# Weights of experts 1 and 2 as casting loads on GpSimd's DMA queue, in place of fp32 staging and GpSimd copies; x group loads issued two units sooner

## The chip, the cores and the metric

The kernel runs on one core of one Trainium2 chip. The metric is device time in microseconds (us); lower is better.

Engine names in the profile: PE is TensorE (matmul), PEld its weight load, DVE is VectorE, ACT is ScalarE, POOL is GpSimd, SP is SyncE, which here does nothing but issue DMAs; "SPq" is the issuing of DMAs on it. "L464" is line 464 of that kernel. From the point where the change deletes or adds lines on, the numbers of the two kernels differ by one or more.

## The reference, cut to what matters

```python
# attention with 8 batches, 8 heads, 512 local + 32 global tokens, head size 64
x = attention output, reshaped to [4352 tokens, 512]   (8 x 544)

logits = x @ w_gate                        # 8 experts
P = np.exp(logits - logits.max())
for _ in range(8):                         # Sinkhorn: needs the logits of ALL tokens
    P /= P.sum(1, keepdims=True) + 1e-09
    P /= P.sum(0, keepdims=True) + 1e-09
    P *= N / E
out = 0
for e in range(8):
    h = np.maximum(x @ w1[e], 0.0)         # w1[e]: 512 x 1024, fp32
    out += P[:, e:e+1] * (h @ w2[e])       # w2[e]: 1024 x 512, fp32
```

The routing `P` mixes all tokens, so nothing that uses it can start before the gate logits of the last token are there.

## The kernel before: the parts that matter

The kernel has four stages. Attention takes roughly the first 185 us. Routing (eight short iterations on VectorE, with one tiny matmul each) follows. Expert 0 is computed without scaling by `P`, so its matmuls need no routing: PE uses them as filling work inside attention and under the routing. After that come two passes over experts 1 to 3 and 4 to 7, in 119 units of 6.2 us by the kernel's own plan.

The attention output goes through DRAM. GpSimd's queue stores it, SP's queue reads it back transposed.

The weights of experts 1 and 2 are loaded under the second half of attention, as fp32 into a staging tile, and GpSimd copies them to fp16. The weights of expert 3 already come by a DMA that casts on the way; in this kernel all such DMAs are issued by GpSimd.

```python
def fetch(e, i, pool):            # 512 KB of fp32 on SP's queue; 3 staging buffers during attention, 2 later
    t = stg[e, i] = pool.tile([P, F], FP32, tag="w0s" if pool is ld else "s", bufs=3 if pool is ld else 2, ...)
    nc.sync.dma_start(out=t, in_=moe_w1[e, P * i : P * (i + 1)])          # or two blocks of w2
def settle(e, i, pool):           # the cast, on GpSimd
    nc.gpsimd.tensor_copy(out=ws[e][0][...], in_=t...)                    # i < 4; two copies for w2

def fetch_cast(e, i, pool):       # expert 3: fp32 in DRAM to fp16 in SBUF in one DMA
    nc.gpsimd.dma_start(out=ws[e][0][...], in_=moe_w1[e, ...])            # i < 4; two such for w2
```

The order of instructions on every engine is decided when the kernel is built, by a small scheduling model in it. The dependency called "seen" (the last load of v has been issued) is only used by that model. It orders the emission and puts no wait into the program.

The softmax here doesn't subtract the row's maximum and nothing guards it: scores larger than these inputs give would overflow.

Of the kernel before, what the change touches and what calls it, by code (L numbers as in the profile page):

```python
# [10 lines left out]
FP32 = mybir.dt.float32  # L11
# [6 lines left out]
def kernel(  # L18
# [13 lines left out]
    nc = tc.nc  # L32
# [4 lines left out]
    F = moe_w1.shape[2]  # L37
    S = Sg + Sl
    NTOK = B * S
    P = 128  # L40
# [33 lines left out]
    Dhalf, FK, DK = D // 2, FT // 2, DP // 2  # L74
# [4 lines left out]
    ws = {}  # L79
# [6 lines left out]
    def new_w(e, i, pool, tag=""):  # L86
        if i == 0:
            ws[e] = [pool.tile([P, 4, DK, F // 2], FP16, tag="w1r" + tag, bufs=1, name="w1r"), None, None]
        elif i == 8:
            ws[e][1] = pool.tile([P, 7, FK, Dhalf], FP16, tag="wb" + tag, bufs=1, name="wb")  # L90
# [61 lines left out]
    def op(eng, us, fn, key, deps=(), alloc=None, uses=(), lat=0.15):  # L152
        o = Op()
        o.eng = eng if isinstance(eng, dict) else {eng: us}
        o.pe = eng == "PE"
        o.fn, o.key, o.deps, o.alloc, o.lat, o.end = fn, key, [x for x in deps if x is not None], alloc, lat, None
        users[o] = [o]
        o.held, o.bw, o.nd = [o], 0.0, 1
        o.act, o.fill, o.after = 0, False, []
        for u in uses:  # L160
            if u is not None:
                users[u].append(o)
                o.deps.append(u)
        pending.append(o)
        return o
# [83 lines left out]
    PEL, DMAL = 0.28, 2.2  # L249
# [3 lines left out]
    ld = tc.alloc_tile_pool(name="ld", bufs=1)  # L253
# [14 lines left out]
    stage, nat, gst, late = {}, {}, {}, {}  # L268
# [288 lines left out]
    for m in range(NM):  # L557
        c = lo[m] - (P * m - WIN)
# [22 lines left out]
    def add_load(b, nm, n, of, key):  # L581
        h0, h1 = H * n // of, H * (n + 1) // of
        prev = b - 2 if b == 2 else b - 1
        deps = [] if b < 2 else [ops_cast[prev, nm, i] for i in range(parts_of(nm))]
        ops_load[b, nm, n] = dma(dma_us[nm] / of, lambda: load(b, nm, h0, h1), key, deps)
# [108 lines left out]
    for nm_ in ("q", "k"):  # L694
        add_load(1, nm_, 0, 1, 3.5)

    w0s = {}

    def load_w0(i):
# [21 lines left out]
    for b in range(B):  # L721
# [23 lines left out]
        for g, (t0, n) in enumerate(groups):  # L745
            if S_tok * b < P * (t0 + n) <= S_tok * (b + 1):
                k = HP * (b + 1) + 0.5
                if g >= GPE:
                    TG[g] = dma(2.0, lambda g=g: turn_group(g), k, [x for x in stored[b] + (stored[b - 1] if b else [])],
                                alloc=("xT", 4), lat=5.0, issue=1.4)  # L750
# [17 lines left out]
    for n, (kind, g, i) in enumerate(seq):  # L768
        key = 1000.0 + n
        if kind == "h":  # L770
            us = 0.435
            if i == 0:
                htag = op("NONE", 0.0, lambda: None, -5, w0[:4], alloc=("hT", 2))
            u0 = op("PE", us, lambda g=g, i=i: h_unit(g, i, 0), key, [*w0[:4], before, *BK[g]],
                    alloc=("mm", 2), uses=[TG[g]])
# [6 lines left out]
        else:  # L782
            prev = None
            for q in range(4):
                prev = op("PE", 0.435, lambda g=g, i=i, q=q: y_unit(g, i, q), key,
                          [before, *w0[4:], *([hops[g, f][1] for f in range(FT * groups[g][1] // GT)] if q == 0 else [prev])],
                          alloc=("mm", 2) if q == 0 else None, uses=[hops[g, 0][2]], lat=PEL if q == 3 else 0.0)
# [23 lines left out]
    opened = op("NONE", 0.0, open_late, -5, [psum])  # L811
# [44 lines left out]
    def load_group(n, g):  # L856
        x = xgs[n, g] = late["cp"].tile([P, 2, D], FP16, tag="xg", bufs=3, name="xg")
        nc.sync.dma_start(out=x, in_=xd[256 * g : 256 * (g + 1)].rearrange("(a p) d -> p a d", p=P))
# [24 lines left out]
    def take_x(eng, k):  # L883
        xps[k] = late["cp"].tile([P, DP, 256], FP16, tag="xp", bufs=5, name="xp")
        copy_on(eng, xps[k], xts[k])
# [82 lines left out]
    TU, SEMA = 6.2, 0.12  # L968
    OP = {("open", 0): opened, ("psum", 0): psum, ("routed", 0): chain[-1], **{("y", i): yops[0, i] for i in (0, 1)}}

    def mk(name, u, eng, us, fn, at, deps=(), uses=(), alloc=None, lat=None, bw=0.0):
        if lat is None:
            lat = {"PE": PEL, "NONE": 0.0}.get(eng, SEMA) if isinstance(eng, str) else SEMA
        OP[name, u] = op(eng, us, fn, at, [OP[d] for d in deps if d in OP], alloc, [OP[d] for d in uses if d in OP], lat)
        OP[name, u].bw = bw
# [30 lines left out]
    def add_prep(k):  # L1006
        n, g, e = work[k]
        at = TU * (k - 4.5)
        if e == PASSES[n][0] and ("LG", k) not in OP:
            mk("LG", k, "DMA", 0.45, lambda: load_group(n, g), at - 4 * TU, [("open", 0)], alloc=("xg", 3), lat=4.0, bw=0.8)  # L1010
        for a in (0, 1):
            mk(("SC", a), k, {"ACT": 0.58, "DVE": 0.26}, 0, lambda eng, a=a: scale_x(eng, k, a), at, [("routed", 0)],
               [("LG", k - PASSES[n].index(e))] + [(("SC", 0), k)] * a, alloc=("xs", 2) if a == 0 else None)
        if k < 2:
            mk("PT", k, "PE", 0.45, lambda: flip_x(k), at, [(("SC", 1), k)], [(("SC", 0), k)], ("xt", 1))
            OP["PT", k].act = 0
            mk("TX", k, {"ACT": 0.93, "DVE": 0.61}, 0, lambda eng: take_x(eng, k), at, [], [("PT", k)], ("xp", 5))
        else:
            mk("PX", k, "DMA", 0.45, lambda: put_x(k), at + 1.0, [(("SC", 1), k)], [(("SC", 0), k)], ("xsd", NX), lat=3.0, bw=0.8)
            mk("TX", k, "DMA", 1.25, lambda: turn_x(k), at + TU, [], [("PX", k)], ("xp", 5), lat=3.5, bw=1.2)  # L1020
        for n_ in (2, 3, 4):
            mk(("V", n_), k, "DVE", (0.335, 0.2, 0.2)[n_ - 2], lambda n_=n_: prep(k, n_), TU * (k - 1.5) + 0.01 * n_,
               [(("V", n_ - 1), k)], [("TX", k)], ("tt", 3) if n_ == 2 else None)
# [105 lines left out]
    def store_o(c, a):  # L1129
        nc.gpsimd.dma_start(out=(ya, outr)[c[0]][2 * c[1] + a], in_=obs[c][:, a, :])  # L1130

    stg = {}

    def fetch(e, i, pool):
        t = stg[e, i] = pool.tile([P, F], FP32, tag="w0s" if pool is ld else "s", bufs=3 if pool is ld else 2, name="stg")
        if i < 4:
            nc.sync.dma_start(out=t, in_=moe_w1[e, P * i : P * (i + 1)])
        else:
            nc.sync.dma_start(out=t.rearrange("p (k d) -> p k d", k=2),
                              in_=moe_w2[e, 2 * P * (i - 4) : 2 * P * (i - 3)].rearrange("(k p) d -> p k d", p=P))  # L1140

    def settle(e, i, pool):

        k, t = i % 4, stg[e, i]
        if i < 4:
            new_w(e, i, pool)
            nc.gpsimd.tensor_copy(out=ws[e][0][:, k // DK :: 2, k % DK, :], in_=t.rearrange("p (f x) -> p f x", f=2))
        else:
            if i == 4:
                new_w(e, 8, pool)  # L1150
            for c in (0, 1):
                nc.gpsimd.tensor_copy(out=ws[e][1][:, 2 * c + k // 2, 2 * (k % 2) : 2 * (k % 2) + 2, :],
                                      in_=t.rearrange("p (k c d) -> p c k d", k=2, c=2)[:, c])

    EARLY = 12

    def fetch_cast(e, i, pool):
        k = i % 4
        if i < 4:
            new_w(e, i, pool)  # L1160
            nc.gpsimd.dma_start(out=ws[e][0][:, k // DK :: 2, k % DK, :], in_=moe_w1[e, P * k : P * (k + 1)].rearrange("p (f x) -> p f x", f=2))
        else:
            if i == 4:
                new_w(e, 8, pool)
            for c in (0, 1):
                nc.gpsimd.dma_start(out=ws[e][1][:, 2 * c + k // 2, 2 * (k % 2) : 2 * (k % 2) + 2, :],
                                    in_=moe_w2[e, 2 * P * k : 2 * P * (k + 1), Dhalf * c : Dhalf * (c + 1)].rearrange("(k p) d -> p k d", p=P))

    def load_w_cast(e, pool):
        for i in range(8):  # L1170
            mk(("W", i), e, "POOL", 0.75 if i < 4 else 1.5, lambda i=i: fetch_cast(e, i, pool()), 900.0 + 0.01 * i,
               [("open", 0), (("W", i - 1), e)] + [(("W", i - 3), e)] * (i > 2), lat=3.5)
            if i:
                OP[("W", i), e].deps.remove(OP[("W", i - 1), e])
                OP[("W", i), e].after.append(OP[("W", i - 1), e])
        OP[("WL", 0), e], OP[("WL", 1), e] = OP[("W", 3), e], OP[("W", 7), e]

    def load_w(e, pool):
        for i in range(8):
            early = 8 * (e - 1) + i < EARLY  # L1180
            mk(("W", i), e, "DMA", 0.45, lambda i=i, early=early: fetch(e, i, ld if early else late["ec"]), 900.0 + e + 0.01 * i,
               [("seen", 0) if early else ("open", 0), (("W", i - 1), e) if i else (("W", 7), e - 1)], alloc=("w0s", 3) if early else ("stg", 2), lat=DMAL, bw=1.6)
            mk(("WC", i), e, "POOL", 0.95 if i < 4 else 1.1, lambda i=i: settle(e, i, pool()), 900.0 + e + 0.01 * i, [(("WC", i - 1), e)], [(("W", i), e)])
            if early:
                opened.deps.append(OP[("WC", i), e])
        OP[("WL", 0), e], OP[("WL", 1), e] = OP[("WC", 3), e], OP[("WC", 7), e]

    OP["seen", 0] = ops_load[B - 1, "v", 0]
    c0 = (0, 0)
    for e, pool in ((1, lambda: wA), (2, lambda: late["wD"]), (3, lambda: late["wB"])):  # L1190
        (load_w if e < 3 else load_w_cast)(e, pool)
    for e in (1, 2, 3):
        for n in range(4):
            mk(("C1", n), e, "DVE", 0.605, lambda e=e, n=n: combine_w1(e, n, late["cp" if e < 3 else "wB"], str(e) if e < 3 else ""),
# [4 lines left out]
    for k in range(5):  # L1199
        add_prep(k)  # L1200
# [61 lines left out]
```

## Time and profile before

| | before |
|---|---|
| median of 3 runs | 990.07 us (987.4 to 991.75) |
| profiled span | 986.6 us |
| PE busy | 960.9 us, 97% of the span |
| PE idle, 130 to 265 us (windows) | 135.00 - 130.91 = 4.1 us |
| transposed loads of xG (gate) and xT (expert 0) to landing, medians | 4.6 and 5.0 us |
| last step of the routing, start | 219.0 us |

First the page's line of PE in the kernel before: busy microseconds, share of the span, number of instructions.

```profile
PE 960.9 (97%) x12918; PEld 824.3 (84%) x12918; DVE 819.7 (83%) x2047; ACT 718.4 (73%) x1379; POOL 209.7 (21%) x406
```

Then its windows: bounds, length, busy time and instructions of each engine, granted TensorE clock (1.00 is full), mean DMA share (the time of packets of all queues over 16 engines' time, so it can pass 1), and GB/s.

```profile
130.00:265.00 135.00, 130.91 (x1456) 81.35 (x1452) 101.74 (x248) 84.19 (x167) 44.08 (x62) 1.00 0.87 225
265.00:375.00 110.00, 110.00 (x1496) 104.23 (x1494) 100.74 (x253) 86.85 (x163) 47.02 (x111) 1.00 0.97 194
375.00:600.00 225.00, 222.74 (x2998) 209.23 (x2996) 198.58 (x498) 179.31 (x336) 51.69 (x115) 1.00 0.86 191
...
150.00:175.00 25.00, 24.41 (x354) 13.87 (x351) 14.94 (x42) 17.54 (x38) 9.20 (x13) 1.00 0.78 203
175.00:200.00 25.00, 24.29 (x233) 12.65 (x234) 17.34 (x44) 13.24 (x29) 8.61 (x12) 1.00 0.85 231
200.00:232.00 32.00, 29.93 (x206) 16.97 (x205) 28.18 (x58) 16.86 (x29) 19.14 (x26) 1.00 1.05 269
```

PE is the bottleneck in every stretch shown, and full between 265 and 375 us.

The last piece is VectorE's timeline while GpSimd casts: two subtractions of the same shape (expert weights are combined once on arrival). GpSimd casts from 220.84 to 223.61 us, so the first stands beside casts for most of its length and the second beside none.

```profile
222.06 2.10 DVE L126 TENSOR_TENSOR w1r<-w1r 128x1024 f16<-128x1024 f16 x1
...
224.34 0.68 DVE L126 TENSOR_TENSOR w1x<-w1x,w1r 128x1024 f16<-128x1024 f16 x1
```

### The profile page before, as it was taken

To read this page: it belongs to the slowest core of one execution; us is meant where nothing else is said; L and a number is where in the kernel's file an instruction comes from. 1 tells how busy PE (TensorE), PEld (TensorE's weight loads), DVE (VectorE), ACT (ScalarE), POOL (GpSimd) and SP (SyncE) were. 2 spreads that over 40 slices of the span, in tenths; PEclk is the share of its full clock that TensorE was granted. 3 is DMA by queue.
4 is the path that set the end of the run, shared out by engine and by line. 5 is a ranking of instruction groups with operands and counts; after the bars stand their busy time and mean duration, and the time that the engine had idled before them with its cause. 6 is when DMAs were issued, how large, how long until landed. Compare 5 with 4: busy or idle time off the path is not lost.

```text
span 986.6 us, 31631 instructions
## 1 busy us (share of the span) xinstructions
PE 960.9 (97%) x12918; PEld 824.3 (84%) x12918; DVE 819.7 (83%) x2047; ACT 718.4 (73%) x1379; POOL 209.7 (21%) x406
## 2 busy tenths in 40 slices
PE   6899999998999999999999999999999999999998
PEld 3555655446999999999999989999999999999997
DVE  6888886689689989878888998888888888888876
ACT  5668676556777877877887787777777777777764
POOL 3411124352144443332320000000000000000000
PEclk9999999999999999999999999999999999999999
DMA  9999696898799998799886985555665555556621
GB/s 288 306 254 286 190 282 195 225 277 213 156 233 181 192 202 182 178 195 182 185 178 167 251 201 138 141 139 141 136 141 140 140 140 142 139 140 141 140 73 44
DMA packets 256098, 179.29 MB, mean 182 GB/s; under 512 B 158288, under 2 KB 236880, under 8 KB 255440
## 3 DMA queue, kind: packets, MB, share of 16 engines
q1 hardware_dynamic: 229872, 126.78, 54.1%
q0 software_dynamic: 24496, 50.09, 20.4%
q8 instruction: 101, 1.65, 0.7%
q10 hardware_dynamic: 1584, 0.39, 0.2%
q14 instruction: 45, 0.37, 0.1%
HBM read 91.24 MB, written 66.06 MB: 159 GB/s over the span
## 4 chain that ended last, share of the span: by engine, by line
PE 81%; DVE 8%; DMA 5%; ACT 3%; issue 3%; POOL 1%; SPq 0%; ACTq 0%; DVEq 0%; POOLq 0%
PE X L908 19%; PE Y L908 9%; PE acc_5045 L946 9%; PE acc_5046 L946 9%; PE acc_5043 L946 9%; PE Z L908 5%; PE py L534 5%; PE ph L518 5%; PE acc_5044 L946 4%; PE pt L302 1%; PE sc L328 1%; DVE h L129 1%; DMA w1r<-wd_7_87 1%; DVE o L129 1%; DMA xp<-xsd_83 1%
## 5 line engine op out<-in xcount | busy, mean ns | idle before, releaser
L922 ACT ACTIVATE h<-h 128x512 f16<-128x512 f16 x357 | 225.3, 631 | 109.9 <-DVE h L129 108.3
L908 PEld LDWEIGHTS <-w1r 128*128 128x128 f16 x3808 | 251.0, 98 | 14.9 <-issue 2.2
L908 PEld LDWEIGHTS <-w1x 128*128 128x128 f16 x2856 | 186.3, 98 | 8.7 <-issue 2.3
L946 PEld LDWEIGHTS <-s 128*128 128x128 f16 x1904 | 168.6, 98 | 12.9 <-issue 0.3
L908 PE MATMUL X<-tt,w1r 128*128 128x128 f16 x1904 | 145.1, 219 | 1.0 <-ACT u2s L919 0.9
L946 PE MATMUL acc_5046<-wb,s 128*128 128x256 f16 x952 | 142.3, 273 | 0.1
L946 PEld LDWEIGHTS <-h 128*128 128x128 f16 x1428 | 127.1, 98 | 9.9 <-issue 0.6
L129 DVE TENSOR_TENSOR h<-u2s,Y 128x512 f16<-128x512 f32 x119 | 81.5, 684 | 51.1 <-PE Y L908 51.1
L129 DVE TENSOR_TENSOR h<-u3s,Y 128x512 f16<-128x512 f32 x119 | 81.1, 682 | 9.4 <-PE Y L908 5.3
L129 DVE TENSOR_TENSOR h<-p1s,Z 128x512 f16<-128x512 f32 x119 | 81.4, 684 | 7.8 <-ACT p1s L919 2.2
L919 ACT COPY p1s<-X 128x512 f32<-128x512 f32 x119 | 69.5, 584 | 25.2 <-PE X L908 22.3
L1130 POOL DMA_DIRECT2D out_dram<-o x32 | 17.5, 547 | 307.0 <-DVE o L129 307.0
L919 ACT COPY u2s<-X 128x512 f32<-128x512 f32 x119 | 68.4, 574 | 16.6 <-PE X L908 16.4
L908 PE MATMUL Y<-tt,w1x 128*128 128x128 f16 x952 | 72.6, 219 | 1.6 <-DVE tt L126 1.0
L908 PE MATMUL Z<-xp,w1r 128*128 128x128 f16 x952 | 72.6, 219 | 1.3 <-DVE h L129 1.2
L866 ACT ACTIVATE xs<-xg,P_nat 128x512 f16<-128x512 f16 x100 | 71.8, 723 | 1.6 <-DMA xsd_81<-xs 1.6
L129 DVE TENSOR_TENSOR s<-h 128x512 f16<-128x512 f16 x119 | 50.1, 421 | 27.1 <-ACT h L922 27.0
L908 PE MATMUL X<-tt,w1x 128*128 128x128 f16 x952 | 72.6, 219 | 0.0
L908 PE MATMUL X<-xp,w1r 128*128 128x128 f16 x952 | 72.6, 219 | 0.0
L908 PE MATMUL Y<-xp,w1x 128*128 128x128 f16 x952 | 72.6, 219 | 0.0
L919 ACT COPY u3s<-X 128x512 f32<-128x512 f32 x119 | 68.7, 577 | 4.4 <-PE X L908 3.3
L946 PE MATMUL acc_5045<-wb,h 128*128 128x256 f16 x476 | 71.4, 273 | 0.4 <-DVE o L129 0.4
(725 smaller groups left out, 1902.7 us busy)
## 6 DMA issues: line engine op xcount, KB each, us to landing
y0d<-ys SPq DMA_DIRECT2D x34, 256.0 KB, 5.6
xg<-xd SPq DMA_DIRECT2D x34, 256.0 KB, 3.9
o<-y0d POOLq DMA_DIRECT2D x34, 256.0 KB, 4.5
ya<-o POOLq DMA_DIRECT2D x34, 256.0 KB, 3.2
o<-ya POOLq DMA_DIRECT2D x34, 256.0 KB, 4.0
stg<-in_moe_w_dram SPq DMA_DIRECT2D x16, 512.0 KB, 5.5
out_dram<-o POOLq DMA_DIRECT2D x32, 256.0 KB, 2.7
qs<-in_q_l_dram SPq DMA_DIRECT2D x7, 1024.0 KB, 7.9
```

The source lines that it names most:

```text
L129: nc.vector.tensor_tensor(out=o, in0=a, in1=b_, op=ALU.add)
L302: nc.tensor.transpose(pt[:, j, P * so : P * (so + 1)], nat[b, nm][:, so, 2 * hp : 2 * hp + 2, :], identity)
L328: nc.tensor.matmul(pss[p, m // 2, i][:, off[m] : off[m] + wid[m]], qkT[p][rr, 1, P * m : P * (m + 1)], qkT[p][rr, 0, lo[m] : hi[m]], start ...
L518: nc.tensor.matmul(phs[g, n][:, j], w1_0[:, dk, P * (w * n + j) : P * (w * n + j + 1)], xTs[g][:, dk, 0:TG], start=(dk == 0), stop=(dk == ...
L534: nc.tensor.matmul(pys[g, c], hTs[g][:, fk, P * c : P * (c + 1)], w2_0[:, fk, :], start=(fk == 0), stop=(fk == FT - 1))
L866: nc.scalar.activation(out=o, in_=i, func=AF.Copy, scale=w)
L908: nc.tensor.matmul(dst[:, j, :], l[:, d, P * j : P * (j + 1)], r[:, d, :], start=(first and j == 0 and d == 0), stop=(j == FK - 1 and d == ...
L919: nc.scalar.copy(out=d[k], in_=X[k])
L922: nc.scalar.activation(out=hq(k, f, t), in_=hq(k, f, t) if src is None else src, func=AF.Relu)
L946: nc.tensor.matmul(acc(i), l[:, j, :], wb[:, r, j, :], start=(e == es[0] and j == 0 and i in (1, 5)), stop=(e == es[-1] and j == FK - 1), ...
L1130: nc.gpsimd.dma_start(out=(ya, outr)[c[0]][2 * c[1] + a], in_=obs[c][:, a, :])
```

## The change

The intent: the casts are done by the DMA in flight, as for expert 3. The fp32 staging and 24 GpSimd copies go away, VectorE is no longer disturbed by them, and SP has 16 fewer loads to issue. Separately, the x group loads of the expert passes get an earlier key (the number by which the scheduling model orders the instructions).

```diff
-    def fetch(e, i, pool):      ... nc.sync.dma_start(out=t, in_=moe_w1[e, ...])        # fp32, staged
-    def settle(e, i, pool):     ... nc.gpsimd.tensor_copy(out=ws[e][0][...], in_=t...)
-    EARLY = 12
     ...
-    def load_w_cast(e, pool):
+    def load_w(e, pool):
         for i in range(8):
-            mk(("W", i), e, "POOL", 0.75 if i < 4 else 1.5, lambda i=i: fetch_cast(e, i, pool()), 900.0 + 0.01 * i,
-               [("open", 0), (("W", i - 1), e)] + [(("W", i - 3), e)] * (i > 2), lat=3.5)
+            mk(("W", i), e, "POOL", 0.75 if i < 4 else 1.5, lambda i=i: fetch_cast(e, i, pool()), 900.0 + e + 0.01 * i,
+               [("seen" if e < 3 else "open", 0), ((("W", i - 1), e) if i else (("W", 7), e - 1))] + [(("W", i - 3), e)] * (i > 2), lat=3.5, bw=1.6)
     ...
-    def load_w(e, pool):        ... fetch on "DMA" with alloc=("w0s", 3) or ("stg", 2), then settle on "POOL"
     ...
-        (load_w if e < 3 else load_w_cast)(e, pool)
+        load_w(e, pool)
     ...
-            mk(("LG", k), ..., lambda: load_group(n, g), at - 4 * TU, ...)
+            mk(("LG", k), ..., lambda: load_group(n, g), at - 6 * TU, ...)
```

More of the change, by code (lines that the diff above doesn't have):

```diff
@@ L1009, in add_prep @@
         if e == PASSES[n][0] and ("LG", k) not in OP:
-            mk("LG", k, "DMA", 0.45, lambda: load_group(n, g), at - 4 * TU, [("open", 0)], alloc=("xg", 3), lat=4.0, bw=0.8)
+            mk("LG", k, "DMA", 0.45, lambda: load_group(n, g), at - 6 * TU, [("open", 0)], alloc=("xg", 3), lat=4.0, bw=0.8)
         for a in (0, 1):
@@ L1130, in store_o @@
         nc.gpsimd.dma_start(out=(ya, outr)[c[0]][2 * c[1] + a], in_=obs[c][:, a, :])
-    stg = {}
-    def fetch(e, i, pool):
-        t = stg[e, i] = pool.tile([P, F], FP32, tag="w0s" if pool is ld else "s", bufs=3 if pool is ld else 2, name="stg")
-        if i < 4:
-            nc.sync.dma_start(out=t, in_=moe_w1[e, P * i : P * (i + 1)])
-        else:
-            nc.sync.dma_start(out=t.rearrange("p (k d) -> p k d", k=2),
-                              in_=moe_w2[e, 2 * P * (i - 4) : 2 * P * (i - 3)].rearrange("(k p) d -> p k d", p=P))
-    def settle(e, i, pool):
-        k, t = i % 4, stg[e, i]
-        if i < 4:
-            new_w(e, i, pool)
-            nc.gpsimd.tensor_copy(out=ws[e][0][:, k // DK :: 2, k % DK, :], in_=t.rearrange("p (f x) -> p f x", f=2))
-        else:
-            if i == 4:
-                new_w(e, 8, pool)
-            for c in (0, 1):
-                nc.gpsimd.tensor_copy(out=ws[e][1][:, 2 * c + k // 2, 2 * (k % 2) : 2 * (k % 2) + 2, :],
-                                      in_=t.rearrange("p (k c d) -> p c k d", k=2, c=2)[:, c])
-    EARLY = 12
     def fetch_cast(e, i, pool):
@@ L1176, in load_w_cast @@
         OP[("WL", 0), e], OP[("WL", 1), e] = OP[("W", 3), e], OP[("W", 7), e]
-    def load_w(e, pool):
-        for i in range(8):
-            early = 8 * (e - 1) + i < EARLY
-            mk(("W", i), e, "DMA", 0.45, lambda i=i, early=early: fetch(e, i, ld if early else late["ec"]), 900.0 + e + 0.01 * i,
-               [("seen", 0) if early else ("open", 0), (("W", i - 1), e) if i else (("W", 7), e - 1)], alloc=("w0s", 3) if early else ("stg", 2), lat=DMAL, bw=1.6)
-            mk(("WC", i), e, "POOL", 0.95 if i < 4 else 1.1, lambda i=i: settle(e, i, pool()), 900.0 + e + 0.01 * i, [(("WC", i - 1), e)], [(("W", i), e)])
-            if early:
-                opened.deps.append(OP[("WC", i), e])
-        OP[("WL", 0), e], OP[("WL", 1), e] = OP[("WC", 3), e], OP[("WC", 7), e]
     OP["seen", 0] = ops_load[B - 1, "v", 0]
```

## The prediction

> **What bounds the kernel.** TensorE: the page gives PE 961 of 986.6 us (97%), and the chain of waits is 81% PE. From 250 us on, the windows view shows PE busy 125.0 of 125, 222.7 of 225 and 300.0 of 300 us at clock 1.00. The PE idle time left lies at the start (14 us in the first 75), at the end (5 us), and around the hand-over from attention and routing to the expert passes: 1.3 us in 150-200, 2.1 in 218-232, 0.7 in 232-250. The changed code runs from about 131 us on, so it can reach these 4 us and the 2.3 us in 375-600.
>
> **Removed.** 16 fp32 loads of 512 KB on SP (5.5 us to landing) and 24 GpSimd casts (8 x 1.15 and 16 x 0.70 us, 147-231 us). GpSimd is 21% busy; what the casts cost is VectorE time: in the timeline two combine steps last 1.13 and 2.10 us between 220.9 and 224.2 while GpSimd casts at 220.8-223.6; undisturbed ones take 0.68. Beside other casts: 1.25 instead of 0.68 and 1.27 instead of 0.44 near 189; 0.79 and 0.98 instead of 0.44 near 204 and 211. Together some 4 us. This agrees with the Trainium skill, "SBUF — State Buffer", section "Who interferes with whom": a VectorE instruction with two SBUF inputs contends with a GpSimd instruction that reads SBUF. One combine also waits 1.07 us for a cast (186.2).
>
> **Added.** 24 casting DMAs on GpSimd's queue, 0.71 us of issue each in the trace: 17 us, about what the casts took. Expert 3's, issued in a burst, landed in 8.8 us (w1) and 13.4 us (w2). The new ones start near 132 us, between the stores of attention output on the same queue. A store behind them may land a few us later and delay a transposed load, but there are 10 us gaps, and PE has expert 0's matmuls to fill with until 246 us.
>
> **x loads.** With both programs built, SP's order after the hand-over is the same apart from one swap, and PE's last 9,785 of 12,912 matmuls stand in the same order. Only the first two loads (near 202 us) move up. Buffers, not the key, place the others, so VectorE's 8.6 us of waits for x (8 waits) stay. I expect nothing from this part.
>
> **Critical path.** Routing ends 3 to 4 us sooner than 219.5 us, but PE is filled then, so that alone gains nothing. The gain is PE's idle time in 218-232: two waits for VectorE of 1.0 us (transformed x, sum h), both behind slowed combines. I expect 1 to 1.5 us of 2.1 back, perhaps 0.3 before 200 us, nothing after 250 us: about -1.5 us (0.15%), within the spread of the three runs.
>
> Predicted: 988.5 us, 8 in 10 within 983 to 993. Faster by over 2%: 1%; within 2%: 98%; slower by over 2%: 1%.
>
> **Right if** combines after 131 us take 0.68 us; routing's last step is near 216 us; PE idle in 200-250 falls from 2.8 to about 1.5 us; PE busy after 250 us and the x waits stay.
>
> **Wrong if** casting DMAs hold up the attention stores so long that fill work runs out before 246 us, or starve the last batch's loads; or if the hand-over hides slack in "busy" PE [...], which would bring up to 4 us.

## More of the kernel before

(The comments with line numbers are added; `...` marks cuts.)

```python
def store_x(b, hh):                                   # L423, GpSimd's queue
    nc.gpsimd.dma_start(out=xd[...], in_=xns[2 * b + hh]...)
def store_xg(b):                                      # L428, four small ones
    for hq in range(4):
        nc.gpsimd.dma_start(out=xd[...], in_=ogs[b][Sg * hq : Sg * (hq + 1)])

def turn_group(g):                                    # L444, SP's queue: 512 tokens, for expert 0
    nc.sync.dma_start_transpose(out=xTs[g], in_=xd[P * t0 : P * (t0 + n)])
def turn_gate(g):                                     # L449, SP's queue: for the gate logits, g = 4, 5, 6
    nc.sync.dma_start_transpose(out=xGs[g], in_=xd[P * t0 : P * (t0 + n)])

def gate(g):                                          # L464
    ... nc.tensor.matmul(pl[...], x[:, dk, ...], w_gate_sb[:, dk, :], ...)
# expert 0, the filling work: L518 (ph <- w1, xT), L534 (py <- w2, hT), then a copy of py to the
# tile ys (three buffers, L275) and its store to y0d on SP's queue (L545)
```

The DMA engines are far from idle: their share is 0.78 to 1.05 while attention ends.

The next lines are the gate's transposed loads (tile xG): the time that their issue held SP (nanoseconds, minimum/median/maximum) and the time from issue to landing.

```profile
L449 SPq DMA_TRANSPOSE xG<-xd x3: 2166/2487/2626, 139.4 to 173.2; - x3
...
DMA to landing us min/median/max: 4.5/4.6/4.8
```

The order on SP's queue around the last of them, in the timeline (start, duration, queue, line, what), is the second thing to keep:

```profile
171.10 2.00 SPq L444 DMA_TRANSPOSE xT<-xd  x1
173.15 2.49 SPq L449 DMA_TRANSPOSE xG<-xd  x1
175.74 0.52 SPq L1139 DMA_DIRECT2D stg<-in_moe_w_dram  x1
```

The fp32 weight load (stg) stands on the same queue as the transposes and behind them, and the three staging buffers, which the xG tiles share, limit how many are under way.

## The result, and the profile after

| | before | after |
|---|---|---|
| median of 5 runs each | 989.81 us (987.4 to 991.75) | 1014.72 us (1012.62 to 1019.48) |
| ratio after to before | | 1.0264 (95%: 1.0226 to 1.0302) |
| profiled span | 986.6 us | 1010.9 us |
| PE busy, same 12,918 matmuls | 960.9 us | 968.2 us |
| PE idle over the span | 25.7 us | 42.7 us |
| PE idle, 130 to 265 us | 4.1 us | 135.00 - 112.60 = 22.4 us |
| last step of the routing | 219.0 us | 247.4 us |

A ratio here, and in all experiments, is the mean time of one kernel's fast runs over the mean of the other's fast runs of the same rounds; it is therefore not quite the ratio of the medians.

The kernel became 2.6% slower. The page's line and the same windows, after:

```profile
PE 968.2 (96%) x12918; PEld 827.4 (82%) x12918; DVE 816.5 (81%) x2044; ACT 719.7 (71%) x1382; POOL 203.2 (20%) x406
```

```profile
130.00:265.00 135.00, 112.60 (x1232) 64.83 (x1230) 80.32 (x203) 70.14 (x143) 38.73 (x58) 0.91 0.98 167
265.00:375.00 110.00, 109.28 (x1422) 100.17 (x1420) 96.12 (x242) 83.91 (x157) 37.72 (x90) 1.00 0.87 185
375.00:600.00 225.00, 223.23 (x3013) 210.23 (x3010) 197.12 (x490) 177.16 (x331) 57.13 (x134) 1.00 0.92 195
...
150.00:175.00 25.00, 22.82 (x343) 14.01 (x344) 14.23 (x39) 14.86 (x34) 9.67 (x15) 0.93 0.97 157
175.00:200.00 25.00, 13.88 (x207) 7.56 (x205) 9.10 (x29) 9.63 (x23) 7.24 (x12) 0.87 1.30 145
200.00:232.00 32.00, 24.56 (x136) 11.47 (x137) 13.71 (x30) 9.60 (x19) 13.75 (x21) 0.79 1.24 186
```

The loss lies between 130 and 265 us. Before that, and from 265 us on, PE's idle time is as before to within 1.3 us. PE is idle 18.3 us longer there (22.4 against 4.1). PE's busy time over the whole span grew by 7.3 us for the same matmuls, because the granted clock was lower; 1.2 us of that fell in the first 75 us, where the change has no part (60.75 against 61.99 us, clock 1.00 against 0.95). Idle time over the whole span grew by 17.0 us. The two together, 17.0 + 7.3, are the 24.3 us by which the profiled span grew.

Look also at the DMA columns of 175 to 200 us: the share rose from 0.85 to 1.30, and the bytes moved fell from 231 to 145 GB/s. The DMA engines had more packets in hand and got less done.

What PE waited for, in 130 to 260 us (engine, line, who released it: total, times, longest). In the kernel before, the wait for xG is 0.6 us and the longest wait of any kind 1.0 us. After:

```profile
PE pl L464 <- DMA xG<-xd: 13.6, 2, 11.4
PE ph L518 <- ACT ys L275: 7.2, 1, 7.2
PE ph L518 <- DMA xT<-xd: 1.6, 1, 1.6
```

The gate's transposed loads in the kernel after:

```profile
L449 SPq DMA_TRANSPOSE xG<-xd x3: 3792/5732/10552, 143.1 to 180.1; - x3
...
DMA to landing us min/median/max: 9.0/10.2/20.1
```

One landed 20.1 us after its issue, where 4.6 us was usual. The transposes for expert 0 (xT) went from 4.0/5.0/6.7 to 7.4/14.7/16.9 us in the same way. Why then is seen by putting GpSimd's queue beside SP's queue. First GpSimd, then SP, after:

```profile
170.36 0.77 POOL L423 DMA_DIRECT2D xd<-xn  x1 [8.81 <-DVE rg L405]
171.12 2.17 POOL L428 DMA_DIRECT2D xd<-og  x4
173.15 2.85 POOL L1137 DMA_DIRECT2D w1r<-in_moe_w_dram  x4
180.51 0.76 POOL L423 DMA_DIRECT2D xd<-xn  x1 [4.51 <-DVE rg L405]
181.27 2.83 POOL L1142 DMA_DIRECT2D wb<-in_moe_w_dram  x4
```

```profile
174.53 5.52 SPq L444 DMA_TRANSPOSE xT<-xd  x1
180.10 10.55 SPq L449 DMA_TRANSPOSE xG<-xd  x1
190.74 1.82 SPq L545 DMA_DIRECT2D y0d<-ys  x2
...
205.58 10.24 SPq L444 DMA_TRANSPOSE xT<-xd  x2
215.92 2.22 SPq L545 DMA_DIRECT2D y0d<-ys  x3
```

GpSimd sits at an attention store until VectorE has normalised that part of the batch (8.81 us). When that store goes out, the casting loads behind it in the program have nothing to wait for and go out at once, four in 2.85 us. The transposes wait for the same stores to land. So a burst of weights is on its way when the transposes are released: here the burst starts at 173.15 us and the transposes at 174.53 and 180.10. The second of them, the longest xG load, then also meets the next burst (181.27), which stands behind the first store of the last batch. It repeats at the other stores, with bursts of three or four loads at 134.6, 147.3, 158.7, 173.2 and 181.3 us.

The stores were not what was late for this load: the one at 170.36 landed after 2.6 us, the four from 171.12 on after 1.7 to 2.0 us each. The transpose itself was slow, and it held SP's queue for 10.55 us. Two stores of expert 0's results (y0d) stood behind it. The stores of the last batch, however, were late: those at 180.51 and 189.51 us, behind or among the bursts, landed after 17.2 and 14.5 us, where the same two took 5.3 and 4.7 us before. No xG load waited for them, but the last two xT loads did (third loss below).

Here is what PE made of that, in its timeline after:

```profile
188.28 0.59 PE L534 MATMUL py<-w_0_76,hT 128*128 128x512 f16 x2
200.26 0.59 PE L464 MATMUL pl<-w_gate_sb,xG 128*128 128x8 f16 x16 [11.38 <-DMA xG<-xd]
...
201.21 1.87 PE L534 MATMUL py<-w_0_76,hT 128*128 128x512 f16 x4
...
204.15 3.26 PE L518 MATMUL ph<-xT,w_0_75 128*128 128x512 f16 x8
207.25 1.89 PE L534 MATMUL py<-w_0_76,hT 128*128 128x512 f16 x8
```

There was filling work for PE: the py matmuls at 201.21 started with no wait. But PE ran its instructions in the order in which they were emitted, and there the gate's matmuls come first, because the scheduling model planned an earlier landing. (The kernel gives the model 0.8 us of start, 2.0 of transfer and 5.0 of latency for such a load, so 7.8 us at least, and more when it counts other transfers ahead. Printed while building the two kernels, the plan for the last xG load is 9.1 us from issue to landing before and 11.8 after; the transfers took 4.8 and 20.1 us.) Nor did the load go out as planned: 1.4 us after the xT transpose ahead of it by the plan, 5.6 us (174.53 to 180.10) in the run. PE therefore stood 11.38 us in front of 16 matmuls that take 0.59 us.

Three losses follow:

- Four py matmuls took 1.87 us just after the wait, and eight ph matmuls 3.26 us, where eight took 1.89 us three microseconds later. The Trainium skill, page "TensorE: Matmul & The Clock Gate", section "What's actually happening", says that the array's clock falls back to half after an idle window of about 3.4 us and needs about as long under load to return. The trace agrees with the fall: 11.4 us of idling, then matmuls at about half rate. The return took longer here than the page's time, about 7 us (200.26 to 207.25). The mean clock of 0.79 in the window of 200 to 232 us is made of this stretch (0.50 and 0.51 in 200 to 207 us) and of one after the 7.2 us wait below (0.66 in 222 to 232 us).
- The last gate matmul started at 203.3 us in place of 184.3 us, so routing began 19 us later. It ended 28.4 us later (247.4 against 219.0), since VectorE in the routing also waited 17.8 us in place of 5.2 us for its small matmuls on PE (L842, L841 before), some of which stood behind the next loss.
- The last two xT transposes, released late by the last batch's stores (at 205.58 us in place of 191.92), went out next to expert 3's burst of loads and held SP for 10.24 us. The y0d stores behind them landed late (11.3 us), the three ys buffers stayed full, and PE waited 7.2 us for one.

### The profile page after: what moved, and what is told of

The parts are those of the page before. It is cut to its first block, busy times and chain, and to the rows that moved or that the text cites. A ratio compares the mean times of both kernels' runs of the same rounds, so it can differ in the third digit from the quotient of the medians.

```text
span 1010.9 us, 31615 instructions
## 1 busy us (share of the span) xinstructions
PE 968.2 (96%) x12918; PEld 827.4 (82%) x12918; DVE 816.5 (81%) x2044; ACT 719.7 (71%) x1382; POOL 203.2 (20%) x406
## 3 DMA queue, kind: packets, MB, share of 16 engines
HBM read 91.24 MB, written 66.06 MB: 156 GB/s over the span
## 4 chain that ended last, share of the span: by engine, by line
PE 86%; DMA 6%; DVE 5%; ACT 2%; issue 1%; SPq 0%; POOL 0%; ACTq 0%; DVEq 0%; POOLq 0%
PE X L909 20%; PE Y L909 10%; PE acc_5013 L947 10%; PE acc_5014 L947 10%; PE acc_5011 L947 10%; PE py L534 5%; PE Z L909 5%; PE ph L518 5%; PE acc_5012 L947 5%; DMA xG<-xd 3%; PE pt L302 1%; DMA y0d<-ys 1%; PE sc L328 1%; DMA w1r<-wd_7_87 1%; DMA xg<-xd 1%
## 5 line engine op out<-in xcount | busy, mean ns | idle before, releaser
L909 PEld LDWEIGHTS <-w1r 128*128 128x128 f16 x3808 | 251.0, 98 | 13.7 <-issue 2.3
L518 PE MATMUL ph<-xT,w_0_75 128*128 128x512 f16 (+1 forms) x288 | 72.0, 376 | 9.5 <-ACT ys L275 7.2
L920 ACT COPY u2s<-X 128x512 f32<-128x512 f32 x119 | 68.3, 574 | 17.1 <-PE X L909 16.9
```

The source lines that it names most:

```text
L518: nc.tensor.matmul(phs[g, n][:, j], w1_0[:, dk, P * (w * n + j) : P * (w * n + j + 1)], xTs[g][:, dk, 0:TG], start=(dk == 0), stop=(dk == ...
L909: nc.tensor.matmul(dst[:, j, :], l[:, d, P * j : P * (j + 1)], r[:, d, :], start=(first and j == 0 and d == 0), stop=(j == FK - 1 and d == ...
L920: nc.scalar.copy(out=d[k], in_=X[k])
```

## The experiments

The theories, under the names that the expectations use:

- SHARE: the transposes go through the same 16 DMA engines as every other queue's transfers, and any burst of bulk loads from another queue stretches them. In the kernel before, the weight loads stood behind the transposes on SP's own queue and in small number.
- MIX: the same slowing, but special to casting loads on GpSimd's queue.
- QUEUE: the attention stores stand behind casting loads on GpSimd's queue, so the transposes are released late.
- XLOAD: the earlier x group loads are to blame, alone or with the rest.

All times below are medians with their range and the number of runs; the ratio is to the kernel before in the same rounds.

| run | median us (range, runs) | ratio to before (95%) | xG to landing, min/median/max us | routing's last step at, us |
|---|---|---|---|---|
| x_only | 988.4 (987.83 to 991.25, 4) | 1.0001 (0.9976 to 1.0026) | 4.4/4.9/5.0 | 220.9 |
| cast_only | 1013.52 (1012.09 to 1014.67, 4) | 1.0249 (1.0230 to 1.0267) | 8.9/9.2/22.3 | 249.8 |
| stores_sp | 1020.42 (1016.36 to 1021.85, 4) | 1.0312 (1.0284 to 1.0341) | 4.5/4.7/6.3 | 257.2 |
| held | 987.23 (986.17 to 988.34, 4) | 0.9962 (0.9927 to 0.9996) | 4.6/7.0/11.5 | 224.7 |
| cap1 | 990.96 (988.62 to 994.55, 4) | 1.0002 (0.9962 to 1.0043) | 4.7/6.0/9.5 | 218.8 |
| late | 1000.18 (995.62 to 1003.92, 4) | 1.0077 (1.0029 to 1.0125) | 4.6/6.8/6.9 | 231.6 |
| fp32_pool | 996.56 (991.98 to 998.77, 4) | 1.0050 (1.0007 to 1.0093) | 4.9/7.1/7.8 | 219.2 |
| stores_sp_paced | 1009.81 (1007.22 to 1010.21, 4) | 1.0211 (1.0190 to 1.0232) | 6.9/9.2/9.3 | 242.2 |
| before_stores_sp | 987.84 (986.49 to 989.97, 4) | 1.0001 (0.9976 to 1.0026) | 4.4/4.5/4.5 | 221.4 |
| held_again | 984.68 (983.02 to 987.22, 6) | 0.9964 (0.9945 to 0.9984) | 4.4/6.0/12.7 | 224.3 |

Two further runs, micro and micro2, are small kernels that measure the disputed cost by itself.

### The two parts of the change, one at a time

x_only is the kernel before with the x loads' new key alone; cast_only is the kernel after with the old key.

```diff
 # x_only, against the kernel before; cast_only is this edit undone in the kernel after
-            mk("LG", k, ..., at - 4 * TU, ...)
+            mk("LG", k, ..., at - 6 * TU, ...)
```

> The kernel before with only the x group loads two units sooner. Theories: MIX (casting loads in flight and the DMA transposes of the attention output slow one another), QUEUE (the attention stores wait behind casting loads in GpSimd's queue), XLOAD (the two first x loads, now ahead of the last transposes on SP, hold them up). MIX and QUEUE expect 990 us, within 2 us of before, xG landing in 4.7 us. XLOAD expects the whole loss, about 1010 us or more.

> The changed kernel with the x loads put back to four units ahead. MIX and QUEUE expect 1014 us, within 5 us of the changed kernel, and xG landing in 10 to 20 us. XLOAD expects 988 us.

Measured: x_only takes the time of the kernel before (1.0001), cast_only the loss (1.0249 against 1.0264 for both parts, with overlapping intervals), with xG landing after up to 22.3 us. The x loads do nothing, for good or bad. XLOAD falls, and the casting loads carry the loss.

### The attention stores on SP's queue

stores_sp is the kernel after, with the stores of attention output taken off GpSimd's queue, so that no store can stand behind a casting load.

```diff
-        nc.gpsimd.dma_start(out=xd[...], in_=xns[2 * b + hh]...)      # store_x
+        nc.sync.dma_start(out=xd[...], in_=xns[2 * b + hh]...)
-            nc.gpsimd.dma_start(out=xd[...], in_=ogs[b]...)           # store_xg
+            nc.sync.dma_start(out=xd[...], in_=ogs[b]...)
```

> The changed kernel with the stores of attention output on SP's queue, so that no casting load is ahead of them in their queue. QUEUE expects the loss to vanish: about 990 us, xG landing in about 5 us. MIX expects most of the loss to stay: over 1005 us, and xG still landing in 10 us or more.

Measured: 1.0312, slower still, and neither theory's forecast: xG landed as QUEUE had it, the time was as MIX had it. The run doesn't answer its question, because the edit took away a wait that I had overlooked: it was the stores on GpSimd's queue, waiting for VectorE, that spaced the casting loads out. Freed of them, GpSimd issued the casting loads of experts 1 and 2 between 81 and 114 us. The loads of q that attention was waiting for landed after 15.9 us (median, 75 to 130 us) in place of 8.1, and PE was busy 40.62 us of those 55, where the kernel before has 54.70. The xG transposes, later and with no weight burst beside them, were at their old 4.7 us. So the run tells two things: the damage follows the burst to wherever the burst is, and it hits plain loads on SP's queue as well as transposes. The question about QUEUE had to be asked again (below).

### The cost by itself

micro is a small kernel with a wrong result (it has the reference's output shape and none of its arithmetic). Each phase issues four weight loads of 512 KB and two 512 x 512 transposes, either alone or together, and waits for all before the next.

```python
for what in (["T"], ["gc"], ["gp"], ["gc", "T"], ["gp", "T"], ["ap", "T"], ["sp", "T"]):
    # T: two transposes on SP; gc: casting loads on GpSimd; gp: plain loads on GpSimd;
    # ap: plain loads on ACT's queue; sp: plain loads on SP's own queue, ahead of T
```

> Another program (its output is wrong on purpose): in phases, two DMA transposes of 512x512 on SP alone; four casting loads of 128x1024 fp32 to fp16 on GpSimd's queue alone; four plain fp32 loads there alone; and the two transposes beside casting loads, beside plain loads on GpSimd's queue, beside plain loads on ACT's queue, and behind plain loads on SP's own queue; three times over. MIX expects transposes to land in about 5 us alone and in 10 us or more beside casting loads, and in less than 9 us beside plain ones. If any other queue's traffic slows them alike (theory SHARE), the plain loads on GpSimd's and ACT's queue slow them as much as the casting ones. QUEUE expects no great difference, under 8 us in all.

Measured, over the three repetitions: transposes alone landed after 4.5 to 4.7 us (one of 12.3 us in the first phase ran beside the program's opening stores). Beside four casting loads they took 7.6 to 10.0 us, beside four plain loads on GpSimd's queue 8.3 to 10.8 us, beside four plain loads on ACT's queue 13.1 to 17.3 us. Behind four loads on SP's own queue the first took 8.0 to 9.3 and the second 4.4 to 4.5 us. So it isn't the cast: plain loads do the same, and those of ACT's queue do worse. MIX falls. SHARE stands in the main, though its "alike" doesn't hold for ACT's queue.

### Keeping the casting loads, and spacing them out

Three edits of the kernel after keep all 24 casting loads and change only when they go out. held lets each burst wait for the transposes that are released with it (a one-column GpSimd copy of the tile is the wait). cap1 lets each piece (one load of w1, or the two half-sized loads of a w2 block) wait until the piece before has landed. late moves all of them behind attention.

```diff
 # held
+            n = 8 * (e - 1) + i
+            hold = n // 4 + 4 if n < 16 and n % 4 == 0 else None      # every fourth piece of experts 1, 2
+            def piece_w(i=i, hold=hold):
+                if hold is not None:
+                    v = xGs[hold] if hold < 7 else xTs[8]
+                    wait_for(v[:, 0, 0:1])                            # GpSimd copies one column
+                fetch_cast(e, i, pool())
 ...
 # cap1
+                if e < 3 and wq:
+                    wait_for(wq[-1])                                  # a column of the piece before
 # late
-               [("seen" if e < 3 else "open", 0), ...
+               [("open", 0), ...
```

> The changed kernel, but each burst of casting loads waits until the transposed loads of its batch have landed (a one-column copy on GpSimd that reads the transposed tile). Theory SHARE: a burst of loads in another queue shares the 16 DMA engines with the transposes and stretches them, and PE then waits for the last xG. SHARE expects xG back at 4 to 6 us, no PE wait for xG over 2 us, and 985 to 994 us. QUEUE (stores behind casting loads) expects the loss to stay in part, over 1000 us, since the next batch's stores still follow a burst in the queue.

> The changed kernel with at most one piece of the casting loads of experts 1 and 2 outstanding (each waits for the landing of the one before it), at no fixed distance from the transposes. SHARE expects transposes of 5 to 8 us and 988 to 1000 us. If the mere presence of casting loads beside transposes is what costs (MIX), xG stays at 10 us or more and the time over 1005 us.

> The changed kernel with all casting loads after the attention stage. SHARE expects xG at about 5 us and no PE wait for it; the weights of 12 MB then have to come between 187 and about 245 us, beside the last two transposes, so experts 1 and 2 may be a little late: 986 to 998 us. QUEUE expects the same, so this run only bounds what the early loads cost.

Measured: with held the whole loss is gone (0.9962), and PE's wait for xG fell from 13.6 to 1.9 us. With cap1 it is gone as well (1.0002; its wait for xG is 0.3 us, and one wait of 6.2 us for a ys buffer remains). The same casting loads, with the same bytes and on the same queue, cost nothing when each burst waits for the transposes before it, or when only one piece is under way. This is the main proof: what these edits have in common is the moment of the loads. They also shift PE's order a little, since the scheduling model sees them (and held adds a dependency to the model's opening of the late buffers). That isn't what helped: ahead of the last xG load's gate matmuls stand 304 of expert 0's matmuls in the kernel before, 314 in the kernel after, 314 in held and 306 in cap1, counted in the traces, so the kernel after had no less work there than the others.

Two parts of the expectations were missed. held did not bring xG back to 4 to 6 us: one landed after 7.0 and one after 11.5 us, because the burst released by the first xG load (three loads at 147.84 us and one at 153.71) met the second one, issued at 151.46 us. It cost little, because the plan of this kernel allows that load 11.5 us. In cap1 one xG load took 9.5 us, where 5 to 8 had been expected.

late missed its expectation (1.0077). The gate's transposes were well (6.9 us at most) and the routing ended at 231.6 us, but the burst then met the last two xT transposes. They held SP from 188.23 us for 11.38 us, the y0d stores stood behind, and PE waited 9.4 us for a ys buffer. It is the third loss of the kernel after, moved: a burst behind attention is still beside something that PE needs.

fp32_pool asks the reverse: the kernel before, whose staged fp32 loads are moved from SP's queue to GpSimd's, in the program and in the model's list, and nothing else. No cast in flight, at most three loads under way.

```diff
-            nc.sync.dma_start(out=t, in_=moe_w1[e, P * i : P * (i + 1)])
+            nc.gpsimd.dma_start(out=t, in_=moe_w1[e, P * i : P * (i + 1)])
```

> The kernel before with its plain fp32 staging loads issued on GpSimd's queue in place of SP's; copies and buffers as before. MIX (casting needed for the loss) expects 990 us, within 3, with xG at 5 us. SHARE expects transposes stretched where they meet loads (xG 6 to 10 us) but only three buffers' worth outstanding, so 992 to 1005 us. QUEUE expects the attention stores, which now stand behind plain loads, to land late and the time to rise to over 1000 us.

Measured: 1.0050, with xG at 4.9/7.1/7.8 us in place of 4.5/4.6/4.8. Plain loads on the other queue stretch the transposes too, by a little under half of what the bursts did in the median (7.1 against 10.2 us, from 4.6), and the staging buffers kept it at that. Landings of 7 to 8 us left PE with only 0.6 us of waiting for xG, as before. The run's 0.5% is hardly outside its interval; its largest new wait is one of 3.0 us for VectorE. A landing of up to some 8 us is nearly free in all these runs, which fits the plan's 7.8 us or more. What costs is the long tail, since the filling work ahead of the gate's matmuls covers only so much.

### The stores again, with the spacing kept

stores_sp_paced repeats stores_sp, but GpSimd still waits, by one-column copies, where the stores stood. The casting loads keep their moments to within some 3 us, and no store stands behind them. before_stores_sp is the control: the kernel before with its stores on SP's queue.

```diff
 # stores_sp_paced: the edit of stores_sp, and
+            op("POOL", 0.75, lambda: [wait_for(xns[2 * b + hh][:, 3, i, 0:1]) for i in range(4)], k + 0.5, ...)
+                op("POOL", 2.2, lambda: wait_for(ogs[b][:, 1, 0:1]), k + 0.5, ...)
```

> Mends stores_sp, where GpSimd, freed of the stores, ran ahead and issued the casting loads 50 us earlier. Here the stores are on SP's queue too, but GpSimd still waits for the same attention results where the stores stood (one-column copies), so the casting loads start when they do in the changed kernel and no store stands behind them in their queue. QUEUE expects xG back near 5 us and a time within 5 us of the control below. SHARE expects xG of 9 us or more and at least 12 us above the control.

> Control: the kernel before with the attention stores on SP's queue. Both theories expect what SP's longer order costs by itself, 988 to 1000 us, with xG at about 5 us.

Measured: with no store behind any casting load the kernel still loses 2.1% (1.0211; the interval, 1.0190 to 1.0232, is clear of no loss but spans the 2% at which a run counts as slower, so that verdict is unclear), and the control loses nothing (1.0001). The landing of xG in stores_sp_paced, then in the control:

```profile
DMA to landing us min/median/max: 6.9/9.2/9.3
```

```profile
DMA to landing us min/median/max: 4.4/4.5/4.5
```

QUEUE falls as the main cause. It seems to have a small part: in the kernel after, GpSimd's last two small stores of the last batch waited 6.63 and 1.20 us for earlier DMAs of its own queue, at 198 and 199.7 us; the large stores of that batch landed after 17.2 and 14.5 us, against 7.4 and 6.1 us in stores_sp_paced; and stores_sp_paced is a little better than the kernel after. Its longest xG landing is also shorter, 9.3 us against 20.1 us. No run separates those two, so how much of the remaining half per cent is due to which stays open. Most of its loss sits in the other waits: 7.5 us for a ys buffer, 3.8 us for xG, 2.9 us for xT.

### How the backlog sets the landing, and the better version once more

micro2 varies the number of loads ahead of the two transposes, the queue they are on, and whether they stand ahead or behind. held_again repeats held in five rounds.

```python
# (queue, number of 512 KB loads, L: loads emitted first / T: transposes emitted first / -: no transposes)
for a in (("", 0), ("gc", 1), ("gc", 2), ("gc", 4), ("gc", 8), ("gp", 4), ("gp", 8),
          ("sp", 4, "L"), ("sp", 4, "T"), ("gc", 8, "-"), ("gp", 8, "-")):
```

> The separate program again (wrong output on purpose): two DMA transposes of 512x512 beside a backlog of 0, 1, 2, 4 and 8 casting loads of 512 KB read on GpSimd's queue, 4 and 8 plain loads there, 4 plain loads ahead of them and 4 behind them on SP's own queue, and 8 loads of both kinds alone. SHARE expects the landing of the second transpose to grow with the backlog, some 5 us with none and 14 us or more with 8, about as much for plain loads as for casting ones, and to be about 5 us where the loads stand behind the transposes on the same queue. MIX expects plain loads to slow them less than half as much as casting ones.

> The kernel held once more with five rounds, to see whether it beats the kernel before: SHARE together with the freed VectorE time expects 985 to 988.5 us, a ratio to before of 0.995 to 0.999.

Measured in micro2, second of two repetitions (the first agrees within 1.0 us in every row but the first row, where one transpose took 12.3 us beside the program's opening stores):

| beside the two transposes | first, second transpose to landing, us |
|---|---|
| nothing | 4.7, 4.7 |
| 1 casting load on GpSimd's queue | 5.9, 5.7 |
| 2 | 7.6, 7.4 |
| 4 | 7.6, 9.8 |
| 8 | 7.6, 15.3 |
| 4 plain loads on GpSimd's queue | 7.9, 10.4 |
| 8 plain loads on GpSimd's queue | 8.0, 15.1 |
| 4 plain loads on SP's own queue, ahead | 8.1, 4.6 |
| 4 plain loads on SP's own queue, behind | 4.6, 5.0 |

The lines behind the first, fifth, seventh and last row, one fence each; with two transposes the minimum and the maximum are the two of them. Nothing beside them:

```profile
DMA to landing us min/median/max: 4.7/4.7/4.7
```

Eight casting loads:

```profile
DMA to landing us min/median/max: 7.6/11.5/15.3
```

Eight plain loads on the same queue:

```profile
DMA to landing us min/median/max: 8.0/11.5/15.1
```

Four plain loads behind the transposes on the transposes' own queue:

```profile
DMA to landing us min/median/max: 4.6/4.8/5.0
```

The second transpose lands when the backlog is gone: beside eight casting loads at 226.4 us, the last load at 225.2. Eight casting loads alone take 14.0 us from gate to gate. Casting or plain makes no difference (15.3, 15.1). The arrangement does: four loads behind the transposes on SP's own queue cost them 0.3 us, four on GpSimd's queue 5 us. From the first issue to the last landing, four plain loads and two transposes take about the same in all three arrangements (12.3 us with GpSimd's queue, 11.8 ahead and 12.5 behind on SP's), so what changes is which transfer is late. One reservation: the last row doesn't separate the queue from the moment. The issue of the transposes held SP until 273.8 us, so the loads behind them went out from 273.96 us on, when the first transpose was about to land (274.07). This is what the kernel before had: its weight loads were in the last row, and the change moved them to the fourth and beyond.

The Trainium skill states the sharing on its page "DMA: Bandwidth & Descriptors", section "Issuing engines are not separate DMA queues": DMAs of the scalar, sync or gpsimd engine "will ultimately run on the same 16 DMA engines and interleave with each other, regardless of the engine that started them". The runs agree (15.3 against 4.7 us). The section "Queues, rings and completion order" of the same page adds that each DMA engine goes round-robin between the queues that have work for it. That would explain why loads sent from another queue at the same moment stretch a transpose: the engines would take turns between the two. The runs show the effect (4.7 alone, 9.8 to 10.4 us beside four loads), not the order of packets.

held_again gave 0.9964 (0.9945 to 0.9984): 3.5 us faster than the kernel before, and 2.9% faster than the kernel after if the two ratios are set against each other (0.9964/1.0264 = 0.971). It is the fastest version. Its gain over the kernel before is inside the 2% that count as the same, and was found in both runs of it. The window and the routing's last step in held_again:

```profile
130.00:265.00 135.00, 131.29 (x1497) 82.55 (x1497) 97.16 (x248) 84.46 (x170) 41.34 (x66) 1.00 0.91 196
```

```profile
L829 DVE TENSOR_TENSOR P_nat<-st,srv x1: 442/442/442, 224.3 to 224.3; 128x272 f32<-128x272 f32 x1
```

PE is busy 131.29 of 135 us, against 130.91 before and 112.60 after, though the longest xG landing is still 12.7 us here (issued at 150.00 us, beside the burst of 146.57): PE had enough work ahead of that gate, which the plan puts 11.5 us after the issue, and waited 2.9 us in all. The routing ends 5 us later than before without loss, because PE is filled until then.

## Why the prediction was wrong, point by point

| step of the prediction | what the runs showed |
|---|---|
| PE bounds the kernel; the change can reach some 4 us of idle PE time after 130 us | Right for the gain. Wrong as a bound of the effect: the loss came in time in which PE was not idle before. |
| The GpSimd casts slow VectorE's combining of weights (1.13 and 2.10 us for 0.68); without them 0.68 us | Right: in the kernel after they take 0.63 to 0.69 us, with none beside a cast. This agrees with the page "SBUF — State Buffer", section "Who interferes with whom", of the Trainium skill. |
| 24 casting DMAs cost 0.71 us of GpSimd's time each, 17 us in all, about what the casts took | Right as a number (four in 2.85 us, POOL busy 203.2 against 209.7 us), and not the cost that counts. |
| "A store behind them may land a few us later and delay a transposed load, but there are 10 us gaps" | Failed, in cause and size. The stores ahead of the longest xG load landed in 1.7 to 2.6 us; the transposed load was itself stretched, to 20.1 us. The last batch's large stores did land late, but by 10 to 12 us and not "a few" (14.5 and 17.2 us, from 4.7 and 5.3), and released the last two xT loads 13.7 us later. |
| "PE has expert 0's matmuls to fill with until 246 us" | Failed. The work was there, but behind the gate's matmuls in PE's order: 11.4 us of waiting in front of it. |
| Routing's last step near 216 us; PE idle in 200 to 250 us down to 1.5 us | Failed: 247.4 us; PE idle in 200 to 250 us 7.4 us (32.00 - 24.56, and nothing in 232 to 250). |
| x group loads: nothing | Right: x_only 1.0001. |
| Nothing after 250 us | Right in kind: from 265 us on, PE is as full as before (109.28 of 110, 223.23 of 225 us). |

The step that failed is the costing of the added DMAs. The prediction counted what they take from the engine that issues them, and what they may do to the stores on their own queue. It did not count their time on the 16 DMA engines, which the transposes on SP's queue use at the same moment. The old loads moved the same bytes from DRAM (91.24 MB read in both profiles), and so the new ones looked like the same traffic. But the old ones stood behind the transposes on the same queue, three at a time at most, and the new ones went out in bursts of three or four on another queue, right behind the stores that release the transposes.

The evidence was in the profile before. The prediction quotes how long expert 3's casting loads took in a burst (8.8 and 13.4 us to landing), and the DMA share already stood at 0.78 to 1.05 in those windows. I read those landings as a property of casting loads, and did not ask what they would do to others. Asking that would have given an estimate: a burst of four occupies the engines for about 9 us (the 8.8 us), so a transpose that shares them with it lands after 9 to 13 us (8.8 + 4.6) in place of 4.6 us. Against the plan's 9.1 to 11.8 us that would have warned of a wait of some us; it would still have missed most of the 11.4 us, since the longest load met two bursts and went out late behind a slow xT load.

The "wrong if" clause named the fill and the stores. The fill failed by its place in PE's order and not by running out, and the stores were not the main cause; so the clause was near in place and wrong in mechanism.

What stays open: why the rate fell to 145 GB/s in 175 to 200 us while the DMA engines' share rose to 1.30, why one xG took 20.1 us where micro2's longest, with eight loads, took 15.3 us (it met the two bursts, an xT load that landed only at 190.76 us and late stores; no run takes these apart), and the small part that stores behind loads have.

## What to carry to other kernels

Before a load is moved to another DMA queue, ask what it stood behind on the old one, and which short transfers that an engine waits for are released at the same moment on the other queues; count its time on the shared DMA engines and not only its issue. If it must move, give it a wait that lets the urgent transfers land first: here one-column copies on an idle engine turned a loss of 2.6% into 0.4% below the kernel before, which counts as the same. And filling work covers a late load only where it stands ahead of the waiting instruction in the engine's order.

## What the Trainium skill lacked or had wrong

- "DMA: Bandwidth & Descriptors", "Issuing engines are not separate DMA queues": it states that all issuers share the 16 engines, and adds that starting DMAs on several engines only saves issue time. It gives no size for what a short transfer loses by it, nor does the page's account of turns between queues. Here, four 512 KB loads cost two transposes 0.3 us when they stood behind them on the same queue, and 5.1 to 5.7 us when they were sent at the same moment on GpSimd's queue (5.0 against 9.8 and 10.4 us, from 4.7 us alone).
- The same page, on DMA transposes: none of its sections gives the stretch of a transpose beside ordinary loads. The runs show 4.7 us alone, 5.9 us beside one 512 KB load, 9.8 us beside four, 15.3 us beside eight, and up to 20.1 us in the kernel. It says that a transpose next to ordinary DMAs needs nothing, which holds for correctness: every full kernel here gave the right result.
- No page tells of a difference between queues in this: four plain loads on ACT's queue stretched the transposes to 13.1 to 17.3 us, the same loads on GpSimd's queue to 8.3 to 10.8 us (micro).
- No page gives a size for how long a transpose that is slowed by other queues' loads holds the issuing queue: its issue on SP took 2.2 to 2.6 us before and up to 10.55 us after, and what stood behind it (stores of expert 0's results) cost PE 7.2 us.
